# Lower left quarter of the diagonal score blocks read back from memory instead of computed; pairs in a new order, steps of the row work moved

## The chip, the cores and the metric

The kernel runs on one core of one Trainium2 chip. The metric is the device time of one execution in microseconds (us); the median of several runs counts.

## What is computed

For each of 8 batches of 2496 rows: scores of z with itself, squared after a Relu, applied to v, and multiplied by u elementwise. The result x (19968 rows of 256) goes through a mixture of 8 experts, each of which takes at most 80 rows.

```python
scores = (1.0 / S) * np.matmul(z, z.transpose(0, 2, 1))     # 8 x 2496 x 2496
attn = np.maximum(scores, 0.0) ** 2
x = (u * np.matmul(attn, v)).reshape(B * S, D)
logits = x @ w_gate                                        # 19968 x 8
expert_idx = np.argmax(logits, axis=1)                     # gate_w: its softmax share
for e in range(E):                                         # the 80 rows of largest gate_w
    h = np.maximum(x[tok_idx] @ w1[e], 0.0)
    out[tok_idx] = gate_w[tok_idx, None] * (h @ w2[e])
```

The score matrix of a batch is symmetric, since both factors are z.

## The kernel before

The rows of a batch are 20 tiles of 128 (the last holds 64), and five query chunks `qc` of four tiles: 512 columns, 448 in the last. A chunk is worked off against ten key pairs (two tiles of keys each), so a batch is a grid of five by ten steps, and the program is a list of 400 steps `(b, qc, r)`, r being the position in `pairs_of`. For each step `attend` does the products with v: for both tiles of the pair and both halves of the 256 output columns three matmuls (high and low parts, `ah`, `al` of the scores and the two parts of v), all adding into the chunk's accumulators; the batch's last tile needs two of the three. Two steps earlier (`LOOK`), `scores` prepares the pair: where key chunk and query chunk are equal or the keys come later, PE computes them (two matmuls a tile: `zc` and `zd` hold the parts of z), ACT does Relu and square, ACT or DVE casts the high part `ah`, and DVE subtracts for the low part `al`.

Where the key chunk is later, the scores are kept for the mirrored block too. `mirror` transposes 32 by 32 blocks on DVE into a tile `x`, `mirror_out` writes it to memory (`y`, 1 MB for 512 by 512), `mirror_back` reads it transposed at the level of blocks into one of four buffers (`blk`, four DMAs), and `mirrored` takes the high and low parts of a pair from there with a copy on ACT and a subtract on DVE. So only 240 of the 400 pairs are computed; the two pairs of a diagonal block (`k // QT == qc`) always are, in full.

While a chunk runs, `finished` does the row work of the chunk before it, each part at a step number `r` of its own: `chunk_x` multiplies by u at the start, then high, middle and low parts for the logits (`xb`), `chunk_store` (two DMA transposes of x from SP), `chunk_store2` (the write of x), `chunk_logits` and `chunk_sum`, and once per batch the gate (`gate_top`, `gate_sum`), the counts and the table. The same loop loads and prepares z and v of the next batch (`load_z`, `prep_zc`, `load_v`, `prep_v`). PE, ACT, DVE and SP run in the order in which this loop writes their instructions. After the last chunk come the choice of rows and the experts.

The lines on which the steps turn (before):

```python
pairs_of = [list(range(NP)) for qc in range(NQ)]
pairs_of[NQ - 2] = [NP - 2, NP - 1, *range(NP - 2)]
...
nc.tensor.matmul(s[:, :nq], zk, zc[:, :nq], start=True, stop=False)
nc.tensor.matmul(s[:, :nq], zk, zd[:, :nq], start=False, stop=True)
```

Of the kernel before, what the change touches and what calls it, by code (L numbers as in the profile page):

```python
# [25 lines left out]
def attn_moe_kernel(ctx, tc, zT, uT, v, wg, w1, w2, out, seq, cap):  # L26
# [26 lines left out]
    def tt(o, a, b, op):  # L53
        V.tensor_tensor(out=o, in0=a, in1=b, op=op)  # L54
# [172 lines left out]
    nsum = const.tile([P, B + 1], F32, name="nsum")  # L227
    tot = const.tile([P, E, NBLK], F32, name="tot")
    incl = const.tile([P, E, NBLK], F32, name="incl")
# [6 lines left out]
    def zero_out(i, n):  # L236
# [8 lines left out]

    pairs_of = [list(range(NP)) for qc in range(NQ)]
    pairs_of[NQ - 2] = [NP - 2, NP - 1, *range(NP - 2)]
    LOOK, AHEAD = 2, 12
# [7 lines left out]

    to_read = [(b, i, j, (b * NQ + i) * NP + pairs_of[i].index(2 * j) - LOOK)
               for b in range(B) for i in range(NQ) for j in range(i)]
# [20 lines left out]
    def mirror_back():  # L279

        while to_read and free:
# [12 lines left out]
            blk[b, i, j] = m  # L294

    def pair_tile(tag, b, qc, k, dt=F32R, bufs=3):
        return ew.tile([P, 2, CH], dt, tag=tag, name=f"{tag}_{b}_{qc}_{k}", bufs=bufs)
# [17 lines left out]
    def scores(b, qc, k):  # L315

        if k // QT < qc:
            return mirrored(b, qc, k)
        nq = min(CH, seq - qc * CH)
        zc, zd = zc_t[b, qc], zd_t[b, qc]  # L320
        a = pair_tile("a", b, qc, k, F32, 2)
        ss = []
        for h in range(2):
            zk = zc_t[b, k // QT][:, (k % QT + h) * P:(k % QT + h + 1) * P]
            s = ps_s.tile([P, CH], F32, tag="s", name=f"s_{b}_{qc}_{k + h}")
            nc.tensor.matmul(s[:, :nq], zk, zc[:, :nq], start=True, stop=False)  # L326
            nc.tensor.matmul(s[:, :nq], zk, zd[:, :nq], start=False, stop=True)  # L327
            ss.append(s)
        for h, s in enumerate(ss):
            nc.scalar.activation(out=a[:, h, :nq], in_=s[:, :nq], func=AF.Relu)  # L330
        nc.scalar.activation(out=a[:, :, :nq], in_=a[:, :, :nq], func=AF.Square)  # L331
        ah = pair_tile("ah", b, qc, k)
        on_v = k // QT == qc or (qc, k) in ON_V and b > 0
        cp(V if on_v else nc.scalar, ah[:, :, :nq], a[:, :, :nq])
        al = pair_tile("al", b, qc, k)
        tt(al[:, :, :nq], a[:, :, :nq], ah[:, :, :nq], ALU.subtract)
        if k // QT > qc:
            for h in range(2):
                mirror(b, k // QT, qc, k % QT + h, a[:, h])
        a_t[b, qc, k] = (ah, al)  # L340
# [3 lines left out]
    def attend(b, qc, k, cols=range(DC)):  # L344
        nq = min(CH, seq - qc * CH)
        first, last = 2 * pairs_of[qc][0], 2 * pairs_of[qc][-1] + 1
        if k == first:
# [116 lines left out]
    def gate_top(b, q0, q1):  # L464
# [16 lines left out]
        tt(d, lg, bc(mx), ALU.subtract)  # L481
        ex = ex_last[:, q0 * QT:q1 * QT] if last else small("ex")
        nc.scalar.activation(out=ex, in_=d, func=AF.Exp)
# [202 lines left out]
    WARM = 3, 6  # L686
    WARM0 = 8
    steps = [(b, qc, r) for b in range(B) for qc in range(NQ) for r in range(NP)]
    ET = mybir.EngineType
# [31 lines left out]
    def finished(b, qc, r):  # L721
# [4 lines left out]
        elif r == 2:  # L726
            chunk_rest(b, qc)
        if r == (3 if at_end else 1):
            chunk_store(b, qc)
        if r == (5 if at_end else 3):  # L730
            chunk_store2(b, qc)
        if r == (2 if at_end else 3):
            chunk_mid(b, qc)
        if r == (3 if at_end else 4):
            chunk_lo(b, qc)
        if r == (5 if at_end else 6):
            chunk_logits(b, qc)
            chunk_sum(b, qc)
        kb = b * BPB
        if b < B - 1 and qc == NQ - 1:  # L740
            if r == 7:
                gate_top(b, 0, NQ)
            elif r == 8:
                gate_sum(b, gate_near(b, 0), gp)
        elif qc == 0 and b > 0:
            part = kb - BPB, kb
            if r == 2:
                count(*part)
            elif r == 4:
                up_to(*part)  # L750
                blocks(ps_m, "m", gp, oh, *part)
# [13 lines left out]
    with tc.manual_schedule(engines={ET.PE, ET.Activation, ET.DVE, ET.SP}):  # L765
# [11 lines left out]
        for i, (b, qc, r) in enumerate(steps):  # L777
# [4 lines left out]
            if i + LOOK < len(steps):  # L782
                nb, nqc, nr = steps[i + LOOK]
                scores(nb, nqc, 2 * pairs_of[nqc][nr])
            if r == 0 and prev:
                chunk_x(*prev)
            if b == 0 and qc == 0:
# [5 lines left out]
                if r == 8:  # L793
                    constants_v()
            p = pairs_of[qc][r]
            for k in (2 * p, 2 * p + 1):
# [8 lines left out]
            if b + 1 < B:  # L805
                if r == 1:
                    z_raw[b + 1, qc] = load_z(b + 1, qc)
                if r == 5:
                    prep_zc(b + 1, qc, z_raw.pop((b + 1, qc)))
                if qc == NQ - 2 and r in (2, 4):  # L810
                    g = r // 2 - 1
                    v_raw[b + 1, g] = load_v(b + 1, g)
                if qc == NQ - 1:
                    g = (r - 1) // 2 if r < 9 else 4
                    if r in (2, 4, 6, 8, 9):
                        prep_v(b + 1, g, v_raw.pop((b + 1, g)), nc.scalar, V)
                        if g + 2 < NQ:
                            v_raw[b + 1, g + 2] = load_v(b + 1, g + 2)
            if nb < B and r == 1:
                prep_zd(nb, nqc)  # L820
# [6 lines left out]
            mirror_back()  # L827
            mirror_out()
            if r == NP - 1:
                prev = b, qc  # L830
# [580 lines left out]
```

## Time and profile before

| | |
|---|---|
| median of 3 runs (lowest to highest) | 1389.96 us (1388.79 to 1390.28) |
| the profiled execution | 1388.46 us |
| its span, first to last instruction | 1386.6 us |
| PE busy | 1367.1 us, 99% |
| DVE, ACT busy | 1060.6 us (76%), 1008.8 us (73%) |
| mean granted TensorE clock | 0.992 of full |
| DMA | 311.89 MB, mean 225 GB/s |

The span is what the profile sees; the execution is 1.9 us longer. The stream of attention matmuls begins at 10.0 us and ends near 1305; a batch takes 162.0 us of it. In the rows below PE is TensorE, PEld its weight loads, DVE VectorE, ACT ScalarE, SP the engine that issues most DMAs. A row of the timeline gives start, length, engine, line, operation, output and input.

### The profile page before, as it was taken

Reading aid. Unit: us, or ns where it says so; the run is one execution under the profiler, and the core shown is the slowest. Engines: PE = TensorE matmul, PEld = TensorE weight load, DVE = VectorE, ACT = ScalarE, POOL = GpSimd, SP = SyncE. Lnnn points to the kernel's source line nnn. Section 1 sums busy time; section 2 is a strip of 40 time slices with the busy share of each in tenths; the row PEclk is TensorE's granted clock in tenths of the full one; section 3 lists DMA queues with packets and bytes.
Section 4 is the critical chain, followed back from the end, with each engine's and each line's share of the span. In section 5 each row is a group of like instructions: output and inputs, shape, how many; then the busy total and the mean of one; then the engine's idle time right before and its main releaser. Section 6 shows DMA issues by size and latency. Waiting matters only on the chain. (4 is left out here: it accounts for less than half of the span.)

```text
span 1386.6 us, 19562 instructions
## 1 busy us (share of the span) xinstructions
PE 1367.1 (99%) x7087; PEld 1139.5 (82%) x7087; DVE 1060.6 (76%) x1517; ACT 1008.8 (73%) x1282; POOL 36.5 (3%) x57
## 2 busy tenths in 40 slices
PE   9999999999999999999999999999999999999887
PEld 6888888888888888888888888888888888888666
DVE  8876788668877788767886688777787678867785
ACT  8866687758777587666887577775877668876375
POOL 0000000000000000000000000000000000000062
PEclk9999999999999999999999999999999999999989
DMA  6899877995888958997688958889588986789774
GB/s 223 252 249 271 225 204 239 235 267 143 256 237 231 273 151 245 239 261 197 188 252 232 270 143 259 238 225 274 145 246 239 255 210 179 220 229 252 176 225 141
DMA packets 260070, 311.89 MB, mean 225 GB/s; under 512 B 96152, under 2 KB 188192, under 8 KB 249728
## 3 DMA queue, kind: packets, MB, share of 16 engines
q1 hardware_dynamic: 258752, 309.02, 81.4%
q0 software_dynamic: 1216, 1.56, 0.4%
q8 instruction: 57, 0.93, 0.3%
q14 instruction: 45, 0.37, 0.1%
HBM read 153.48 MB, written 126.37 MB: 202 GB/s over the span
## 5 line engine op out<-in xcount | busy, mean ns | idle before, releaser
L359 PE MATMUL acc<-ah,vt 128*128 128x512 f32 (+1 forms) x1520 | 584.5, 385 | 0.3 <-DVE vt L146 0.3
L360 PE MATMUL acc<-al,vt 128*128 128x512 f32 (+1 forms) x1520 | 584.5, 385 | 0.3 <-DVE al L54 0.2
L358 PE MATMUL acc<-ah,vt 128*128 128x512 f32 (+1 forms) x1520 | 584.2, 384 | 0.0
L54 DVE TENSOR_TENSOR al<-a,ah 128x1024 fp32r<-128x1024 f32 (+1 forms) x240 | 291.5, 1214 | 135.4 <-ACT ah L105 125.6
L330 ACT ACTIVATE a<-s 128x512 f32<-128x512 f32 (+1 forms) x480 | 258.4, 590 | 153.9 <-PE s L327 143.8
L359 PEld LDWEIGHTS acc<-ah,vt 128*128 128x128 f32 x1520 | 285.4, 188 | 53.9 <-DVE vt L146 1.2
L358 PEld LDWEIGHTS acc<-ah,vt 128*128 128x128 f32 x1520 | 285.3, 188 | 52.9
L360 PEld LDWEIGHTS acc<-al,vt 128*128 128x128 f32 x1520 | 285.4, 188 | 52.9 <-DVE al L54 1.2
L331 ACT ACTIVATE a<-a 128x1024 f32<-128x1024 f32 (+1 forms) x240 | 253.0, 1054 | 7.6
L310 ACT CAST ah<-blk 128x1024 fp32r<-128x1024 f32 x160 | 167.0, 1049 | 105.6 <-PE acc L359 88.5
L54 DVE TENSOR_TENSOR al<-blk,ah 128x1024 fp32r<-128x1024 f32 x160 | 193.8, 1216 | 56.1 <-ACT ah L310 53.2
L265 DVE STREAM_TRANSPOSE x<-a 128x512 f32<-128x512 f32 x320 | 207.6, 687 | 0.0
L327 PE MATMUL s<-zd,zc 128*128 128x512 f32 (+1 forms) x480 | 186.5, 388 | 0.0
L105 ACT CAST ah<-a 128x1024 fp32r<-128x1024 f32 x153 | 160.9, 1052 | 4.8
L107 DVE CAST ah<-a 128x1024 fp32r<-128x1024 f32 (+1 forms) x87 | 59.2, 681 | 95.6 <-ACT a L331 95.6
L326 PE MATMUL s<-zc,zc 128*128 128x512 f32 x320 | 128.1, 400 | 0.0
L327 PEld LDWEIGHTS s<-zd,zc 128*128 128x128 f32 x480 | 90.3, 188 | 16.3 <-issue 0.5
L326 PEld LDWEIGHTS s<-zc,zc 128*128 128x128 f32 x320 | 60.1, 188 | 11.1
L326 PE MATMUL s<-zc 128*128 128x512 f32 (+1 forms) x160 | 63.5, 397 | 0.0
L388 ACT CAST xb<-xf 128x1024 bf16<-128x1024 f32 (+1 forms) x39 | 40.0, 1026 | 23.4 <-DVE xf L377 23.1
L396 ACT CAST xb<-xr 128x1024 bf16<-128x1024 f32 (+1 forms) x39 | 39.9, 1024 | 15.5 <-DVE xr L54 15.5
L377 DVE SCALAR_TENSOR_TENSOR xf<-acc,ut 128x512 f32<-128x512 f32 (+2 forms) x82 | 50.1, 653 | 0.0
(171 smaller groups left out, 835.9 us busy)
## 6 DMA issues: line engine op xcount, KB each, us to landing
y<-x SPq DMA_DIRECT2D x80, 1024.0 KB
blk<-y SPq DMA_DIRECT2D x320, 256.0 KB
out<-idle SPq DMA_DIRECT2D x40, 512.0 KB
vraw<-v SPq DMA_DIRECT2D x32, 512.0 KB
ut<-uT SPq DMA_DIRECT2D x32, 512.0 KB
xs<-xq SPq DMA_DIRECT2D x32, 512.0 KB
wraw<-w SPq DMA_DIRECT2D x28, 512.0 KB
zd<-zc SPq DMA_DIRECT2D x78, 128.0 KB
```

Of the source, the lines that this page charges most:

```text
L54: V.tensor_tensor(out=o, in0=a, in1=b, op=op)
L105: eng.copy(out=o, in_=i)
L107: eng.tensor_copy(out=o, in_=i)
L265: V.transpose(out=x[:, :, :, t].rearrange("p n k s -> p k n s"), in_=a)
L310: nc.scalar.copy(out=natural(ah), in_=src)
L326: nc.tensor.matmul(s[:, :nq], zk, zc[:, :nq], start=True, stop=False)
L327: nc.tensor.matmul(s[:, :nq], zk, zd[:, :nq], start=False, stop=True)
L330: nc.scalar.activation(out=a[:, h, :nq], in_=s[:, :nq], func=AF.Relu)
L331: nc.scalar.activation(out=a[:, :, :nq], in_=a[:, :, :nq], func=AF.Square)
L358: nc.tensor.matmul(o, vt[:, t, 0, cs], ah, start=k == first, stop=False)
L359: nc.tensor.matmul(o, vt[:, t, 1, cs], ah, start=False, stop=False)
L360: nc.tensor.matmul(o, vt[:, t, 0, cs], al, start=False, stop=k == last)
```

## The change

A diagonal block is symmetric in itself. Of its two pairs the first (tiles 0 and 1 of the chunk as keys) is still computed in full, and the right half of its result, columns 256 on, is the mirror image of the left half of the second pair. `quarter_out` transposes that right half in 32 by 32 blocks on DVE (tile `xd`), `quarter_write` writes it to memory two steps later (`yd`, 0.25 MB), `quarter_back` reads it after step 3 (`md`, four DMAs of 32 partitions, pieces of 128 values), and the second pair computes columns 256 on alone and takes the rest from `md` by a copy on ACT and a subtract on DVE. `xd` and `md` share one buffer. The first block of the first batch and the last block of the last batch are computed whole as before.

A chunk now starts with its first diagonal pair and ends with its second. x's DMA transposes move from step 1 to 4, its write from 3 to 6, the logits from 6 to 7 (not for the last chunk), the gate, the counts and the table by one to five steps. Key chunks of the next batch are loaded one chunk later, and of v's five groups the last is prepared in the next batch's first chunk. `tot` becomes bfloat16, and the exponentials of the gate overwrite the logits.

```diff
     gall = const.tile([P, NCOL - NT + 32], F32, name="gall")
     nsum = const.tile([P, B + 1], F32, name="nsum")
-    tot = const.tile([P, E, NBLK], F32, name="tot")
+    tot = const.tile([P, E, NBLK], BF16, name="tot")
     incl = const.tile([P, E, NBLK], F32, name="incl")
...
-    pairs_of = [list(range(NP)) for qc in range(NQ)]
-    pairs_of[NQ - 2] = [NP - 2, NP - 1, *range(NP - 2)]
+    def whole_block(b, qc):
+        return (b, qc) in ((0, 0), (B - 1, NQ - 1))
+    def order(b, qc):
+        rest = [p for p in range(NP) if p // 2 != qc]
+        if whole_block(b, qc):
+            return list(range(NP))
+        if qc == NQ - 2:
+            rest = rest[-2:] + rest[:-2]
+        return [2 * qc, *rest, 2 * qc + 1]
+    pairs_of = {(b, qc): order(b, qc) for b in range(B) for qc in range(NQ)}
+    HQ = CH // 2
     LOOK, AHEAD = 2, 12
...
             blk[b, i, j] = m
+    quarter = {}
+    def quarter_out(b, qc, a):
+        x = zpool.tile([P, n32, 2, 2, SQ], F32, tag="md", name=f"xd_{b}_{qc}", bufs=1)
+        for t in range(2):
+            V.transpose(out=x[:, :, :, t].rearrange("p n k s -> p k n s"), in_=a[:, t, HQ:])
+        quarter[b, qc] = now[0], x
+    def quarter_write():
+        for (b, qc), (at, x) in list(quarter.items()):
+            if at is not None and at + 2 <= now[0]:
+                y = dram.tile([n32, SQ, n32, 4 * SQ], F32, tag="yd", name=f"yd_{b}_{qc}", bufs=2)
+                nc.sync.dma_start(out=y.rearrange("g p h f -> (g p) (h f)"),
+                                  in_=x.rearrange("p h k t s -> p (h k t s)"))
+                quarter[b, qc] = None, y
+    def quarter_back(b, qc):
+        _, y = quarter.pop((b, qc))
+        m = zpool.tile([P, n32, 2, 2 * SQ], F32, tag="md", name=f"md_{b}_{qc}", bufs=1)
+        for h in range(n32):
+            nc.sync.dma_start(out=m[h * SQ:(h + 1) * SQ].rearrange("p g k f -> p g (k f)"),
+                              in_=y[:, :, h].rearrange("g p f -> p g f"))
+        quarter[b, qc] = None, m
     def pair_tile(tag, b, qc, k, dt=F32R, bufs=3):
...
         nq = min(CH, seq - qc * CH)
         zc, zd = zc_t[b, qc], zd_t[b, qc]
+        diag = k // QT == qc and not whole_block(b, qc)
+        lower = diag and k % QT > 0
+        c0, c1 = (HQ, nq) if lower else (0, CH if diag else nq)
         a = pair_tile("a", b, qc, k, F32, 2)
...
             zk = zc_t[b, k // QT][:, (k % QT + h) * P:(k % QT + h + 1) * P]
             s = ps_s.tile([P, CH], F32, tag="s", name=f"s_{b}_{qc}_{k + h}")
-            nc.tensor.matmul(s[:, :nq], zk, zc[:, :nq], start=True, stop=False)
-            nc.tensor.matmul(s[:, :nq], zk, zd[:, :nq], start=False, stop=True)
+            nc.tensor.matmul(s[:, c0:c1], zk, zc[:, c0:c1], start=True, stop=False)
+            nc.tensor.matmul(s[:, c0:c1], zk, zd[:, c0:c1], start=False, stop=True)
             ss.append(s)
         for h, s in enumerate(ss):
-            nc.scalar.activation(out=a[:, h, :nq], in_=s[:, :nq], func=AF.Relu)
-        nc.scalar.activation(out=a[:, :, :nq], in_=a[:, :, :nq], func=AF.Square)
+            nc.scalar.activation(out=a[:, h, c0:c1], in_=s[:, c0:c1], func=AF.Relu)
+        nc.scalar.activation(out=a[:, :, c0:c1], in_=a[:, :, c0:c1], func=AF.Square)
         ah = pair_tile("ah", b, qc, k)
+        al = pair_tile("al", b, qc, k)
+        if lower:
+            m = quarter.pop((b, qc))[1].rearrange("p n k (t s) -> p k t n s", t=2)
+            def natural(o):
+                return o[:, :, :HQ].rearrange("p k (t n s) -> p k t n s", t=2, s=SQ)
+            nc.scalar.copy(out=natural(ah), in_=m)
+            tt(natural(al), m, natural(ah), ALU.subtract)
         on_v = k // QT == qc or (qc, k) in ON_V and b > 0
-        cp(V if on_v else nc.scalar, ah[:, :, :nq], a[:, :, :nq])
-        al = pair_tile("al", b, qc, k)
-        tt(al[:, :, :nq], a[:, :, :nq], ah[:, :, :nq], ALU.subtract)
+        cp(V if on_v else nc.scalar, ah[:, :, c0:nq], a[:, :, c0:nq])
+        tt(al[:, :, c0:nq], a[:, :, c0:nq], ah[:, :, c0:nq], ALU.subtract)
+        if diag and not lower:
+            quarter_out(b, qc, a)
         if k // QT > qc:
...
         d = d_last if q1 == NQ and last else small("d")
         tt(d, lg, bc(mx), ALU.subtract)
-        ex = ex_last[:, q0 * QT:q1 * QT] if last else small("ex")
+        ex = ex_last[:, q0 * QT:q1 * QT] if last else lg
         nc.scalar.activation(out=ex, in_=d, func=AF.Exp)
...
     WARM = 3, 6
     WARM0 = 8
+    keys_in = {qc: [(qc - 1, 1, 6)] for qc in range(1, NQ)}
+    keys_in[0] = []
+    keys_in[NQ - 1] = [(NQ - 2, 1, 4), (NQ - 1, 4, 7)]
     steps = [(b, qc, r) for b in range(B) for qc in range(NQ) for r in range(NP)]
...
         elif r == 2:
             chunk_rest(b, qc)
-        if r == (3 if at_end else 1):
+        if r == (3 if at_end else 4):
             chunk_store(b, qc)
-        if r == (5 if at_end else 3):
+        if r == (5 if at_end else 6):
             chunk_store2(b, qc)
...
         if r == (3 if at_end else 4):
             chunk_lo(b, qc)
-        if r == (5 if at_end else 6):
+        if r == (5 if at_end else 6 if qc == NQ - 1 else 7):
             chunk_logits(b, qc)
...
         kb = b * BPB
         if b < B - 1 and qc == NQ - 1:
-            if r == 7:
+            if r == 8:
                 gate_top(b, 0, NQ)
-            elif r == 8:
+            elif r == 9:
                 gate_sum(b, gate_near(b, 0), gp)
         elif qc == 0 and b > 0:
             part = kb - BPB, kb
-            if r == 2:
+            if r == 7:
                 count(*part)
-            elif r == 4:
+            elif r == 9:
                 up_to(*part)
...
                 prep_u(b, qc)
             if b + 1 < B:
-                if r == 1:
-                    z_raw[b + 1, qc] = load_z(b + 1, qc)
-                if r == 5:
-                    prep_zc(b + 1, qc, z_raw.pop((b + 1, qc)))
+                for j, load, prep in keys_in[qc]:
+                    if r == prep:
+                        prep_zc(b + 1, j, z_raw.pop((b + 1, j)))
+                    if r == load:
+                        z_raw[b + 1, j] = load_z(b + 1, j)
                 if qc == NQ - 2 and r in (2, 4):
...
                     v_raw[b + 1, g] = load_v(b + 1, g)
                 if qc == NQ - 1:
-                    g = (r - 1) // 2 if r < 9 else 4
-                    if r in (2, 4, 6, 8, 9):
+                    if r in (1, 3, 6, 8):
+                        g = (1, 3, 6, 8).index(r)
                         prep_v(b + 1, g, v_raw.pop((b + 1, g)), nc.scalar, V)
                         if g + 2 < NQ:
                             v_raw[b + 1, g + 2] = load_v(b + 1, g + 2)
+            if b and qc == 0 and r == 3:
+                prep_v(b, NQ - 1, v_raw.pop((b, NQ - 1)), nc.scalar, V)
             if nb < B and r == 1:
...
             mirror_back()
             mirror_out()
+            quarter_write()
+            if r == 3 and not whole_block(b, qc):
+                quarter_back(b, qc)
             if r == NP - 1:
```

What the order of the instructions shows, at three places of the second batch's second chunk (`qc` 1, whose diagonal pairs are tiles 4, 5 and 6, 7).

On PE, the score matmuls of the diagonal block's second pair; `s_1_6` and `s_1_7` are the scores of tiles 6 and 7. Before, between the products of tiles 0, 1 and tiles 2, 3:

```order
L359 MATMUL acc_1_1_3648<-ah_1_0_3580,vt_0_3062 128x512
L360 MATMUL acc_1_1_3648<-al_1_0_3582,vt_0_3062 128x512
L326 MATMUL s_1_6_3662<-zc_1_2286 128x512
L327 MATMUL s_1_6_3662<-zd_1_3341,zc_1_2286 128x512
L326 MATMUL s_1_7_3665<-zc_1_2286 128x512
L327 MATMUL s_1_7_3665<-zd_1_3341,zc_1_2286 128x512
L358 MATMUL acc_1_0_3647<-ah_1_2_3612,vt_0_3062 128x512
```

Of the change, between the products of tiles 14, 15 and tiles 16, 17:

```order
L410 MATMUL acc_1_1_3764<-ah_1_14_3890,vt_3_3348 128x512
L411 MATMUL acc_1_1_3764<-al_1_14_3891,vt_3_3348 128x512
L367 MATMUL s_1_6_3984<-zc_1_2696 128x256
L368 MATMUL s_1_6_3984<-zd_1_3445,zc_1_2696 128x256
L367 MATMUL s_1_7_3987<-zc_1_2696 128x256
L368 MATMUL s_1_7_3987<-zd_1_3445,zc_1_2696 128x256
L409 MATMUL acc_1_0_3763<-ah_1_16_3924,vt_4_3511 128x512
```

The four matmuls moved from the chunk's second step to its eighth and have 256 columns instead of 512.

On DVE, the end of the first chunk and the start of the second; `lg` and `mx` to `oh` are the gate of the finished batch, `al_1_0` the low part of the first mirrored pair of chunk 1, `al_0_18` the last full pair of chunk 0. Before:

```order
L54 TENSOR_TENSOR al_0_18_3545<-a_0_18_3533,ah_0_18_3543 128x1024
L265 STREAM_TRANSPOSE x_4_0_3492<-a_0_18_3533 128x4x4x32 x2
L478 TENSOR_REDUCE mx_0_3561<-lg_2346 128x20
L54 TENSOR_TENSOR d_0_3563<-lg_2346,mx_0_3561 128x160
L486 SCALAR_TENSOR_TENSOR fw_0_3567<-d_0_3563,first_w 128x160
L489 TENSOR_REDUCE mf_0_3569<-fw_0_3567 128x20
L490 TENSOR_TENSOR oh<-fw_0_3567,mf_0_3569 128x10x2x8
L494 MEMSET oh 64x4
L54 TENSOR_TENSOR al_1_0_3582<-blk_1_0_3471,ah_1_0_3580 128x1024
```

Of the change, to the gate's third instruction (`al_1_0` follows right behind the gate, as before):

```order
L54 TENSOR_TENSOR al_0_18_3602<-a_0_18_3591,ah_0_18_3601 128x1024
L276 STREAM_TRANSPOSE x_4_0_3575<-a_0_18_3591 128x4x4x32 x2
L510 TENSOR_REDUCE lg_2426<-pl_4_3621 128x32
L54 TENSOR_TENSOR al_0_2_3660<-md_0_3517,ah_0_2_3659 128x2x256
L107 CAST ah_0_2_3659<-a_0_2_3649 128x2x256
L54 TENSOR_TENSOR al_0_2_3660<-a_0_2_3649,ah_0_2_3659 128x2x256
L107 CAST ah_1_4_3692<-a_1_4_3682 128x1024
L54 TENSOR_TENSOR al_1_4_3693<-a_1_4_3682,ah_1_4_3692 128x1024
L313 STREAM_TRANSPOSE xd_1_3696<-a_1_4_3682 128x2x4x32 x2
L529 TENSOR_REDUCE mx_0_3709<-lg_2426 128x20
L54 TENSOR_TENSOR d_0_3711<-lg_2426,mx_0_3709 128x160
L537 SCALAR_TENSOR_TENSOR fw_0_3714<-d_0_3711,first_w 128x160
```

The lower pair of chunk 0 (`al_0_2`, from `md_0` and from `a_0_2`) and the first diagonal pair of chunk 1 with its transposes (`xd_1`) now stand ahead of the gate.

On SP, the DMAs of the second chunk, up to the first mirrored block of the third. Before:

```order
L427 DMA_TRANSPOSE xq_0_5239<-xf_0_5193 128x8x128 x2
L100 DMA zraw_5242<-zT 128x512
L120 DMA zd_2_5244<-zc_2_4139 64x512
L121 DMA zd_2_5244<-zc_2_4139 64x512
L159 DMA ut_1_5281<-uT 128x2x512
L436 DMA xs<-xq_0_5239 128x8x256
L580 DMA wtab<-wb_5357 80x256
L239 DMA out<-idle 128x4x256
L275 DMA y_2_1_5392<-x_2_1_5261 128x2048
L292 DMA blk_2_1_5478<-y_2_1_5392 32x4x512 x4
```

Of the change:

```order
L321 DMA yd_1_5387<-xd_1_5306 128x512
L100 DMA zraw_5419<-zT 128x512
L120 DMA zd_2_5421<-zc_2_4601 64x512
L121 DMA zd_2_5421<-zc_2_4601 64x512
L159 DMA ut_1_5453<-uT 128x2x512
L330 DMA md_1_5485<-yd_1_5387 32x4x128 x4
L478 DMA_TRANSPOSE xq_0_5518<-xf_0_5368 128x8x128 x2
L286 DMA y_2_1_5522<-x_2_1_5403 128x2048
L239 DMA out<-idle 128x4x256
L487 DMA xs<-xq_0_5518 128x8x256
L303 DMA blk_2_1_5586<-y_2_1_5522 32x4x512 x4
```

The quarter's write and four reads (`yd_1`, `md_1`) are new, and x's transposes stand behind them instead of first.

## Rows read from the trace of the kernel before

**Rows 1.** The page's busy times, us and share of the span.
```profile
PE 1367.1 (99%) x7087; PEld 1139.5 (82%) x7087; DVE 1060.6 (76%) x1517; ACT 1008.8 (73%) x1282; POOL 36.5 (3%) x57
```

**Rows 2.** Batch 3 by chunk: length, busy per engine, clock, DMA share, GB/s.
```profile
495.88:530.60 34.72, 34.72 (x176) 28.67 (x174) 29.16 (x43) 28.65 (x39) 0.00 (x0) 1.00 0.65 180
530.60:564.88 34.28, 34.28 (x176) 28.06 (x175) 29.20 (x52) 27.44 (x37) 0.00 (x0) 1.00 0.85 252
564.88:599.60 34.72, 34.72 (x175) 28.68 (x174) 23.34 (x29) 26.70 (x34) 0.00 (x0) 1.00 0.93 236
599.60:628.88 29.28, 29.28 (x151) 24.18 (x150) 20.27 (x22) 15.27 (x18) 0.00 (x0) 1.00 0.98 274
628.88:657.88 29.00, 29.00 (x163) 26.44 (x162) 22.61 (x25) 21.30 (x27) 0.00 (x0) 1.00 0.72 194
sum 162.00, PE 162.00 PEld 136.04 DVE 124.58 ACT 119.36 POOL 0.00; mean PE 32.40 PEld 27.21 DVE 24.91 ACT 23.87 POOL 0.00
```

**Rows 3.** Timeline of PE, first and last matmul of three runs.
```profile
599.83 0.39 PE L359 MATMUL acc<-ah,vt 128*128 128x512 f32 x1
...
614.79 0.39 PE L358 MATMUL acc<-ah,vt 128*128 128x512 f32 x1
...
1294.79 0.36 PE L359 MATMUL acc<-ah,vt 128*128 128x448 f32 x1
...
1299.86 0.36 PE L359 MATMUL acc<-ah,vt 128*128 128x448 f32 x1
...
1340.05 0.28 PE L1196 MATMUL op<-w2h,hTh 128*80 128x256 f32 x1
...
1342.74 0.28 PE L1196 MATMUL op<-w2h,hTl 128*80 128x256 f32 x1
```

**Rows 4.** Timeline of PEld, loads of 128 and of 80 columns.
```profile
1301.06 0.19 PEld L358 LDWEIGHTS acc<-ah,vt 128*128 128x128 f32 x1
1301.17 0.19 PEld L359 LDWEIGHTS acc<-ah,vt 128*128 128x128 f32 x1
...
1340.05 0.15 PEld L1196 LDWEIGHTS op<-w2l,hTh 128*80 128x80 f32 x1
1340.17 0.15 PEld L1196 LDWEIGHTS op<-w2h,hTl 128*80 128x80 f32 x1
```

**Rows 5.** The page's costliest matmuls, and the idle time before them.
```profile
L359 PE MATMUL acc<-ah,vt 128*128 128x512 f32 (+1 forms) x1520 | 584.5, 385 | 0.3 <-DVE vt L146 0.3
```

**Rows 6.** Groups by shape: busy us, mean ns of one, idle before.
```profile
L54 DVE TENSOR_TENSOR al<-a,ah 128x1024 fp32r<-128x1024 f32 x224 | 274.0, 1223 | 134.2 <-ACT ah L105 125.6 <-DVE ah L107 0.5
L330 ACT ACTIVATE a<-s 128x512 f32<-128x512 f32 x448 | 242.8, 594 | 132.3 <-PE s L327 122.2 <-DVE x L265 8.2
...
L265 DVE STREAM_TRANSPOSE x<-a 128x512 f32<-128x512 f32 x320 | 207.6, 687 | 0.0
...
L310 ACT CAST ah<-blk 128x1024 fp32r<-128x1024 f32 x160 | 167.0, 1049 | 105.6 <-PE acc L359 88.5 <-PE acc L362 9.7 <-DMA blk<-y 5.0
...
L107 DVE CAST ah<-a 128x1024 fp32r<-128x1024 f32 x71 | 49.2, 693 | 84.1 <-ACT a L331 84.1
```

**Rows 7.** Timeline of ACT, DVE and PE in batch 3's first chunk.
```profile
514.20 1.08 ACT L330 ACTIVATE a<-s 128x512 f32<-128x512 f32 x2
...
517.38 1.09 ACT L330 ACTIVATE a<-s 128x512 f32<-128x512 f32 x2
...
514.33 1.22 DVE L54 TENSOR_TENSOR al<-a,ah 128x1024 fp32r<-128x1024 f32 x1 [1.82 <-ACT ah L105]
...
517.64 0.39 PE L358 MATMUL acc<-ah,vt 128*128 128x512 f32 x1
...
529.40 1.23 DVE L54 TENSOR_TENSOR al<-blk,ah 128x1024 fp32r<-128x1024 f32 x1 [0.19 <-ACT ah L310]
...
531.05 0.39 PE L360 MATMUL acc<-al,vt 128*128 128x512 f32 x1
```

**Rows 8.** Waits, of ACT and of SP's queue: us, times, longest.
```profile
ACT ah L310 <- DMA blk<-y: 5.0, 7, 1.7
...
SPq L292 <- DMA y<-x: 179.5, 38, 8.7
```

More of the change, by code (lines that the diff above doesn't have):

```diff
@@ L255, in attn_moe_kernel @@
     now, to_write = [0], []
-    to_read = [(b, i, j, (b * NQ + i) * NP + pairs_of[i].index(2 * j) - LOOK)
+    to_read = [(b, i, j, (b * NQ + i) * NP + pairs_of[b, i].index(2 * j) - LOOK)
                for b in range(B) for i in range(NQ) for j in range(i)]
@@ L345, in attend @@
         nq = min(CH, seq - qc * CH)
-        first, last = 2 * pairs_of[qc][0], 2 * pairs_of[qc][-1] + 1
+        first, last = 2 * pairs_of[b, qc][0], 2 * pairs_of[b, qc][-1] + 1
         if k == first:
@@ L783, in attn_moe_kernel @@
                 nb, nqc, nr = steps[i + LOOK]
-                scores(nb, nqc, 2 * pairs_of[nqc][nr])
+                scores(nb, nqc, 2 * pairs_of[nb, nqc][nr])
             if r == 0 and prev:
@@ L794, in attn_moe_kernel @@
                     constants_v()
-            p = pairs_of[qc][r]
+            p = pairs_of[b, qc][r]
             for k in (2 * p, 2 * p + 1):
```

## The prediction, made before the changed kernel was run

> **What bounds the kernel now.** I read the busy totals first: TensorE (PE) is busy for 99% of the span [rows 1]. That is not proof by itself, since the ends of matmuls are modelled, so I looked for waits. The costliest matmul line, 1520 matmuls, sat idle before them for 0.3 us in all [rows 5]. I then cut one batch of the middle (batch 3) into its five query chunks. PE is busy from edge to edge in each, at granted clock 1.00, while DVE is busy for 124.58 and ACT for 119.36 of the 162.00 us [rows 2]. The DMA engines come nearest to PE there: 0.93 and 0.98 of the third and fourth chunk, but 0.65 and 0.72 of the first and fifth [rows 2]. So the eight batches are a stream of matmuls without gaps, and a microsecond of matmul taken out of it is a microsecond off the span, as long as nothing that feeds PE becomes late.
>
> The rate of that stream comes from starts, since durations overlap: 66 matmuls of 512 columns start between the two rows at 599.83 and 614.79, so one costs 226.7 ns; 25 of 448 columns take 5.07 us, 202.8 ns each; 23 of 256 columns, in the expert part, take 2.69 us, 117.0 ns each [rows 3]. (At 1.00 clock; a step of one pair is 12 accumulating matmuls, 2.72 us, and with four score matmuls 3.63 us.)
>
> **What the change removes from PE.** In 38 of the 40 diagonal blocks the second pair computes only its right part. 31 of these blocks are of 512 columns: four score matmuls each go from 512 to 256 columns. What 256 columns cost behind a load of 128 weight columns no row shows directly. From below: the 117.0 ns of the expert part, whose loads have 80 columns. From above: nothing saved beyond what the 448-column row has, 202.8 ns, if the weight load of 188 ns that the profile gives (0.19 in [rows 4]) has to end before the next matmul starts. I take 120 ns, near the lower end, for two reasons in the rows: two loads of 128 columns start 0.11 us apart (1301.06 and 1301.17), and loads of 80 columns, recorded at 0.15 us, start every 0.12 us, so a recorded load runs on beside the next one [rows 4]. That gives 31 x 4 x (226.7 - 120) = 13.2 us. In seven blocks of the last chunk the pair goes from 448 to 192 columns; by the load spacing that can't be below 107 ns, and I take 112: 7 x 4 x (202.8 - 112) = 2.5 us. Their first pair, on the other hand, now computes 512 columns instead of 448: 7 x 4 x 23.9 ns = 0.7 us back. Sum: 15.1 us (15.6 with 117 and 107; 2.3 with 202.8 throughout).
>
> The number of matmuls stays the same, and so does everything on PE outside the scores; logits and counts only change their step. The first block and the last are computed whole as before, and so are the start and the tail of 80 us after the stream; I cost them at nothing.
>
> **What it adds, and what hides it.** *DVE*, per block: two transposes of 256 columns (half of the 687 ns row each, 0.7 us), one subtract more but both of half size (no change beyond some 0.1 us), a cast of half size (0.3 us less): about 0.5 us [rows 6]. *ACT*: a copy of 512 elements per partition from the mirrored quarter (half of 1049 ns) against halves of two Relu passes of 594 ns and of the square: between 0.6 us less and, if no pass got shorter at all, 0.5 us more [rows 6]. With 37 and 43 us free per batch [rows 2], both lie beside PE on average. Where they don't have slack on average is what counts, so I looked at the two tightest places.
>
> First, the change from the first chunk to the second, where the gate of the finished batch sits on DVE. The low part of that block's first pair ends at 529.40 + 1.23 = 530.63 and PE uses it at 531.05: 0.42 us to spare, the smallest margin of a batch [rows 7]. Between the start of the block's last tile pair and that use PE does one step before, of ten accumulating matmuls (2.27) and four score matmuls (0.91). Now the lower pair and the next diagonal pair stand between on DVE (0.6 + 0.4 + 0.6 and 0.7 + 1.2 + 0.7 = 4.2 us, from [rows 6] and the parts above), but PE does three steps there: 2.27, 3.63 and 2.72, 8.6 us instead of 3.2. The margin grows by 5.4 - 4.2 = 1.2 us.
>
> Second, the last value group's preparation moves into the first chunk's fourth step. It is three ACT copies of 1280 elements together, 1.3 us at the 1049 ns row. ACT starts a pair every 3.18 us there (514.20 to 517.38) against PE's 3.63, so it wins 0.45 us a step, and the pair of that stretch ends its low part at 515.55, 2.1 us before PE's step at 517.64 [rows 7]. 1.3 us fits, and is won back in three steps. If it did not fit, the excess would show in each of seven batches.
>
> *DMA*: per block one write and four reads, 0.25 MB each way; 2.6 MB per batch. The stream moves 36.7 MB per batch in 133.7 us of DMA time (share x length over [rows 2]), 275 GB/s, so 9.5 us more if the small pieces run at that rate and 19 at half of it: 143 to 153 of 160 us. It fits on average, and not in the fourth chunk, which has 0.6 us free; what overflows goes into the fifth, which has 8. What could be late there: the read of the quarter is issued at step 3, used by ACT at step 7 and by PE at step 9. SP stands still at a read whose write hasn't landed: the existing mirror does that 38 times, 4.7 us on average, 8.7 at worst, with two steps in between [rows 8]; the quarter has three steps and a quarter of the bytes, so I expect less. Behind it in SP's queue stand x's transposes, the next z chunk, a zero-fill and the store of x; first to be missed would be z (for the key chunk three steps on), then the mirrored blocks. But the mirrored blocks of a chunk are all used one step later than before (2.4 to 3.6 us), which is more than the 0.5 MB (1.9 us) that now goes ahead of them, and ACT's waits for them were 5.0 us in the whole span [rows 8]. x's transposes, moved to step 4, still have six steps (over 14 us) until the next chunk overwrites x; logits one step later have two until the gate. All of this I cost at nothing.
>
> **The sum.** The profiled execution took 1388.46 us for a span of 1386.6; less 15.1 this gives 1373.4. The median of the runs is 1389.96, 1.5 above that execution, so the median after should be about 1374.9. Its own range is 1372 to 1378.
>
> **Rivals.** *Short matmuls that don't get shorter* (0.08). If a matmul can't start until the 188 ns load is over, 256 columns cost what 448 do, 2.3 us are saved, and the time is 1387.7: no change that can be told. For it: 448 columns at 202.8 ns is 188 plus 15, as if bound by the load. Against it: the 117 ns cadence beside recorded loads of 150. The Trainium skill's page "TensorE: Matmul & The Clock Gate", section "Back-to-back issue gap", gives a sustained roofline of about 131 ns at 512 columns and 81 at 128, from which 256 columns would save only some 33 ns (an estimate by interpolation), 4 us in all. This trace doesn't agree with it: 226.7 ns at 512 columns.
>
> *ACT or DVE eat part of it* (0.13). The place is the first chunk, whose ACT gets 1.3 us more within one step; if pair chains there run late by 1 us beyond the margin, 7 batches cost 7 us and the time is 1382; between 1378 and 1387.
>
> *DMA becomes the bound, slower* (0.07). The place is the fourth and fifth chunk of a batch. If the quarter's write needs the fourteen microseconds that the worst mirror write needed (two steps and 8.7 us) and SP holds back z and the mirrored blocks behind it, PE waits in both chunks. It gains nothing from 1.1 us of wait in each of 14 such chunks and loses beyond it; at 2 us each the time is 1374.9 + 28 = 1403. For it: 0.98 [rows 2]. Against it: 8 us free right behind, and deadlines that moved later too.
>
> **How the numbers follow.** My forecast has 0.72. Within 0.2% (2.8 us) is about what a measurement of this kernel can't tell from no change. Forecast and second rival are faster, 0.85; the first rival is the same, 0.08; the last is slower, 0.07. The range of 8 in 10 takes the forecast and most of the second rival: 1371 to 1386.
>
> **What would show it.** Right: score matmuls of 256 columns starting about 120 ns apart; the five chunks of a batch together 160.0 us instead of 162.0, 1.7 us of it in the first four; PE still busy from edge to edge; ACT's copy of the quarter without waits for DMA. Wrong: 200 ns between these starts; or PE idle before an accumulating matmul, with ACT's copy named as the one that came last and SP waiting at the quarter's read; or idle time in each first chunk, behind the moved preparation of v. The prediction fails if any wait of half a microsecond appears in every block: 38 such waits are worth more than the saving.

## The result and the profile after

The changed kernel takes 1407.0 us (median of 5 runs, 1403.77 to 1408.77), the kernel before 1389.58 beside it: ratio 1.013 (95% interval 1.0118 to 1.0141), so 1.3% slower and clear of the noise, where 1374.9 and faster was predicted. The profiled execution took 1403.77 us for a span of 1402.0, 15.4 more than before.

The page's busy times after, for [rows 1]:

```profile
PE 1364.2 (97%) x7087; PEld 1137.2 (81%) x7087; DVE 1078.8 (77%) x1631; ACT 993.9 (71%) x1320; POOL 37.6 (3%) x57
```

PE's share fell from 99% to 97%: there are gaps now. Batch 3 by chunk, for [rows 2] (same columns):

```profile
500.07:534.35 34.28, 34.28 (x175) 28.39 (x174) 28.84 (x41) 27.87 (x40) 0.00 (x0) 1.00 0.86 250
534.35:573.29 38.94, 36.28 (x180) 29.74 (x179) 30.44 (x53) 28.25 (x38) 0.00 (x0) 0.96 0.66 199
573.29:607.73 34.44, 34.44 (x178) 28.49 (x176) 23.95 (x37) 25.39 (x34) 0.00 (x0) 1.00 0.93 227
607.73:636.61 28.88, 28.88 (x152) 23.90 (x150) 21.18 (x27) 16.11 (x21) 0.00 (x0) 1.00 1.01 277
636.61:664.45 27.84, 27.84 (x159) 25.38 (x158) 22.86 (x28) 19.99 (x25) 0.00 (x0) 1.00 1.04 263
```

Four chunks are shorter than before and full from edge to edge. The second lost 4.66 us: PE is idle for 2.66 of it, and the mean granted clock is 0.96. So the place is known; the timeline of the changed kernel there shows the event, PE first, then DVE and ACT:

```profile
558.83 0.28 PE L367 MATMUL s<-zc 128*128 128x256 f32 x1
558.95 0.28 PE L368 MATMUL s<-zd,zc 128*128 128x256 f32 x1
559.07 0.28 PE L367 MATMUL s<-zc 128*128 128x256 f32 x1
559.19 0.28 PE L368 MATMUL s<-zd,zc 128*128 128x256 f32 x1
...
562.06 0.77 PE L502 MATMUL pl<-wgs,xb 128*128 128x24 bf16 x24
565.48 0.23 PE L588 MATMUL tp<-oh,ones_b 128*128 128x80 bf16 x2 [2.66 <-DVE lg L510]
...
566.68 0.63 PE L409 MATMUL acc<-ah,vt 128*128 128x512 f32 x1
567.11 0.63 PE L410 MATMUL acc<-ah,vt 128*128 128x512 f32 x1
...
562.38 0.38 DVE L112 CAST zc<-zraw 128x512 fp32r<-128x512 f32 x1
562.80 0.69 DVE L54 TENSOR_TENSOR zc<-zraw,zc 64x512 fp32r<-64x512 f32 x1
563.50 0.69 DVE L54 TENSOR_TENSOR al<-md,ah 128x512 fp32r<-128x512 f32 x1
564.11 0.42 DVE L107 CAST ah<-a 128x512 fp32r<-128x512 f32 x1
564.57 0.69 DVE L54 TENSOR_TENSOR al<-a,ah 128x512 fp32r<-128x512 f32 x1
565.18 0.25 DVE L510 TENSOR_REDUCE lg<-pl 128x32 f32<-128x96 f32 x1
...
565.75 0.23 ACT L590 CAST tot<-tp 128x80 bf16<-128x80 f32 x1 [4.03 <-PE tp L588]
```

The logits (`pl`, L502) and the count of the finished batch (`tp`, L588) are both in step 7 of a batch's second chunk now, and both take their PSUM tile (the memory into which matmuls write) from the pool `ps_m`, which has one buffer. So the count's first matmul has to wait until DVE has read the logits (the reduce, L510). That reduce stands in DVE's queue behind the key chunk's preparation and the three operations of the lower pair, and ends at 565.43. PE works in order: all that is behind the count waits too. Afterwards matmuls of 512 columns start 0.427 us apart instead of 0.227, for a while. The windows of the wait and behind it (clock in the third column from the right):

```profile
562.06:565.48 3.42, 0.76 (x26) 0.69 (x25) 3.28 (x7) 0.00 (x0) 0.00 (x0) 1.00 0.88 364
565.48:566.68 1.20, 1.20 (x7) 0.98 (x6) 0.00 (x0) 0.63 (x2) 0.00 (x0) 0.88 0.28 116
566.68:570.43 3.75, 3.75 (x11) 2.95 (x10) 1.76 (x2) 1.89 (x4) 0.00 (x0) 0.58 0.00 0
```

PE was at 2.4 GHz (granted clock 1.00), did nothing for 2.66 us, and then its matmuls came at the pace of 1.2 GHz for some 3.6 us (mean granted clock 0.58 in the last window). The waits of the whole span, for [rows 8] (us, times, longest), and the costliest matmul, for [rows 5]:

```profile
SPq L303 <- DMA y<-x: 75.9, 24, 8.2
...
ACT ah L381 <- DMA md<-yd: 27.2, 15, 5.2
...
PE tp L588 <- DVE lg L510: 17.4, 7, 2.7
```

```profile
L409 PE MATMUL acc<-ah,vt 128*128 128x512 f32 (+1 forms) x1520 | 588.0, 387 | 1.9 <-DVE ah L107 1.9
```

The count's wait comes seven times, once for every batch but the first. The first of two small matmuls at each count carries the wait, and the costly line [rows 5] shows nothing of it: its 1.9 us are another wait, in the last batch.

Two theories stood before the runs below. Theory A: the loss is the wait for the one buffer, and the clock behind the wait. Theory B: the quarter's way through memory makes DVE and ACT late, and the count only shows it.

### The profile page after: what moved, and what is told of

Its sections match the earlier page's. It is cut to its first block, busy times and chain, and to the rows that moved or that the text cites. A ratio compares the mean times of both kernels' runs of the same rounds, so it can differ in the third digit from the quotient of the medians.

```text
span 1402.0 us, 19932 instructions
## 1 busy us (share of the span) xinstructions
PE 1364.2 (97%) x7087; PEld 1137.2 (81%) x7087; DVE 1078.8 (77%) x1631; ACT 993.9 (71%) x1320; POOL 37.6 (3%) x57
## 5 line engine op out<-in xcount | busy, mean ns | idle before, releaser
L54 DVE TENSOR_TENSOR al<-a,ah 128x1024 fp32r<-128x1024 f32 (+1 forms) x240 | 271.2, 1130 | 142.4 <-ACT ah L105 137.8
L371 ACT ACTIVATE a<-s 128x512 f32<-128x512 f32 x480 | 243.3, 557 | 118.1 <-PE s L368 113.6
L372 ACT ACTIVATE a<-a 128x1024 f32<-128x1024 f32 x240 | 237.5, 989 | 7.8
L368 PE MATMUL s<-zd,zc 128*128 128x512 f32 x480 | 179.8, 378 | 0.0
L367 PE MATMUL s<-zc,zc 128*128 128x512 f32 x320 | 124.7, 390 | 0.0
L107 DVE CAST ah<-a 128x1024 fp32r<-128x1024 f32 (+3 forms) x87 | 48.7, 559 | 51.4 <-ACT a L372 51.0
L54 DVE TENSOR_TENSOR al<-md,ah 128x512 fp32r<-128x512 f32 x38 | 26.1, 686 | 42.2 <-ACT ah L381 40.4
L367 PE MATMUL s<-zc 128*128 128x512 f32 (+3 forms) x160 | 58.5, 376 | 0.0
```

Source lines behind the costliest of these rows:

```text
L107: eng.tensor_copy(out=o, in_=i)
L367: nc.tensor.matmul(s[:, c0:c1], zk, zc[:, c0:c1], start=True, stop=False)
L368: nc.tensor.matmul(s[:, c0:c1], zk, zd[:, c0:c1], start=False, stop=True)
L371: nc.scalar.activation(out=a[:, h, c0:c1], in_=s[:, c0:c1], func=AF.Relu)
L372: nc.scalar.activation(out=a[:, :, c0:c1], in_=a[:, :, c0:c1], func=AF.Square)
```

## Experiments

Ratios are to the kernel before, run beside each; brackets are 95% intervals. (7,3) is batch 7, chunk 3. Unless another kernel is named, an edit is one of the changed kernel.

**Count back in step 2.** `if r == 7: count` to `r == 2`, the table from step 9 to 4.

> The changed kernel with one thing undone: the counts of the finished batch go back from step 7 to step 2 of the second chunk, their sums and table from step 9 to step 4. Theory A (the counts' matmuls wait for the one PSUM buffer that the logits of the same step hold until DVE has summed them, 2.7 us a batch, and the granted clock falls behind the wait, 1.4 us more; about 4 us in each of seven batches): the wait goes, the second chunk takes about 35.0 us instead of 38.9, the time is 1376 to 1381, below the kernel before. Theory B (the quarter's way through memory keeps DVE and ACT late, and the counts only show it): PE waits as long elsewhere, the time stays at 1400 or above.

Measured: 1378.7 us, ratio 0.9927 [0.9915, 0.9939]. The second chunk takes 35.07 us in batch 3.

**Count one step after the logits.** `if r == 7: count` to `r == 8`.

> The changed kernel, the counts one step later (8 instead of 7), sums and table at 9 as in the change. Theory A: one step is 2.7 to 3.6 us, and DVE's sum of the logits ended 2.5 us after the logits' last matmul, so the counts find the buffer free or nearly so: at most 0.5 us of wait a batch, the time is 1376 to 1384. Theory B: as before, 1400 or above.

Measured: 1377.29 us, 0.9919 [0.9904, 0.9933]; second chunk 34.66, batch 3 160.10 us. With the count in step 2 and in step 8 alike it starts without a wait in all seven batches, as theory A has it.

**No quarter.** `diag = False`, no `quarter_back`: lower pairs computed whole, all else of the change kept.

> The changed kernel without the mirrored quarter: the second diagonal pair is computed whole, so there are no transposes for it, no write, no reads; the order of pairs and all moved steps stay. Theory A: the 15 us of score columns come back and the wait of the counts stays (DVE has the same work ahead of the logits' sum, to 0.1 us), so the time is 1415 to 1425. Theory B: without the transfers the stall is gone, and the time is that of the kernel before, 1387 to 1393.

Measured: 1403.41 us, 1.0116 [1.0094, 1.0138]. Without any quarter the kernel is still slow, so B is not the loss. But it was less than expected of A: the wait is 1.87 us in four batches, and behind a wait that long the clock stayed at 1.00. The wait is shorter from both sides: in batch 3, counted from the start of the second chunk, PE comes to the logits at 28.11 us instead of 27.71 and DVE ends the reduce at 30.68 instead of 31.08. The lower pair's own work on DVE isn't shorter: from its first operation to the reduce 1.94 us, against 1.68 with the quarter. In batches 1 and 6 the wait is 2.2 us; the clock fell behind the first of these and not behind the second. The windows behind the count in batches 1, 2 and 6:

```profile
237.38:241.38 4.00, 4.00 (x14) 3.16 (x14) 0.95 (x2) 2.37 (x4) 0.00 (x0) 0.65 0.01 2
402.90:406.90 4.00, 4.00 (x19) 3.34 (x19) 0.94 (x2) 3.06 (x5) 0.00 (x0) 1.00 0.02 4
1058.74:1062.74 4.00, 4.00 (x19) 3.32 (x19) 0.94 (x2) 3.03 (x5) 0.00 (x0) 1.00 0.02 8
```

**The kernel before, with only the collision.** In the old kernel: logits from step 6 to 7, count from 2 to 7, table from 4 to 9.

> The kernel before with only this moved: logits of all but the last chunk from step 6 to 7, counts from step 2 to 7, sums and table from 4 to 9. Nothing of the quarter, old order of pairs, old place of x's transposes. Theory A: the counts wait behind the logits here too (DVE has a subtract and two transposes ahead of the sum, 2.4 us), with the clock's fall some 3 to 4.5 us in seven batches, so the time is 1408 to 1421. Theory B: no quarter, no stall: 1388 to 1392.

Measured: 1409.55 us, 1.0147 [1.0132, 1.0162]. This alone makes a slowdown of 20.7 us, in a kernel without any of the quarter. In batches 1 and 2, windows of the wait and of the 4 us behind it:

```profile
235.80:237.99 2.19, 0.01 (x2) 0.00 (x0) 2.13 (x4) 0.00 (x0) 0.00 (x0) 1.00 1.02 313
237.99:241.99 4.00, 4.00 (x13) 3.15 (x13) 1.22 (x1) 1.19 (x2) 0.00 (x0) 0.60 0.80 166
401.63:403.82 2.19, 0.00 (x1) 0.00 (x1) 2.13 (x4) 0.00 (x0) 0.00 (x0) 1.00 0.99 352
403.82:407.82 4.00, 4.00 (x19) 3.34 (x19) 1.28 (x2) 2.24 (x3) 0.00 (x0) 1.00 0.91 190
```

Equal waits, but 13 matmuls behind the one and 19 behind the other: these second chunks take 37.98 and 36.36 us. The fall of the clock costs 1.6 us of its own where it comes, in four of the seven batches.

**The wait filled with matmuls on idle data.** Behind the logits of each first chunk, which PE computes during the second:

```diff
+        if qc == 0 and b > 0:
+            for _ in range(14):
+                nc.tensor.matmul(pl[:, P:], idle[:, :P], idle[:, :CH - P], start=True, stop=True)
```

> The changed kernel, with 14 matmuls of 384 bf16 columns on idle data placed on PE behind the logits of each second chunk's hold (the count in step 7 still waits for the reduce of the logits, and nothing is left out of the computation; the added matmuls write PSUM columns that nobody reads). They should take some 2.2 to 2.4 us, about as long as PE's wait in the changed kernel. The theory that the loss is the wait plus a clock that falls behind it: the wait stays as long in sum, the granted clock in the stretch behind the count stays at 1.00, the matmuls there stand 0.227 us apart in place of 0.427, and each of the seven batches wins 1.4 to 2.0 us: 1391 to 1397 us. The rival, that the whole loss is the wait and what must be caught up behind it: the second chunk stays at 38 to 39 us and the time at 1403 to 1409 us.

Measured: 1395.16 us, 1.0055 [1.0039, 1.007]. Timeline of PE:

```profile
558.01 2.44 PE L507 MATMUL pl<-idle 128*128 128x384 bf16 x14
560.80 0.23 PE L591 MATMUL tp<-oh,ones_b 128*128 128x80 bf16 x2 [0.36 <-DVE lg L513]
...
561.87 0.39 PE L409 MATMUL acc<-ah,vt 128*128 128x512 f32 x1
562.10 0.39 PE L410 MATMUL acc<-ah,vt 128*128 128x512 f32 x1
```

The count starts as late as before, the matmuls behind it stand 0.23 us apart, the chunk takes 37.31 us, 1.63 less than in the changed kernel. So the wait and the clock are two costs, and this is the first alone.

**A buffer of its own**, that is, one of the three of the scores' pool, which the logits don't use. `tp = ps_m.tile(..., tag="m")` in `count` to `ps_s.tile(..., tag="s")`; step 7 kept.

> The changed kernel, count left in step 7, but its PSUM tile taken from the pool of the scores (three buffers) in place of the pool that the logits use (one buffer). If the loss is that one buffer is shared by the logits and the count: PE no longer waits for the reduce (0 of the 2.66 us), the second chunk takes 34.6 to 35.3 us, and the time is 1376 to 1381 us, as with the count in another step. If the count's step 7 is in itself the trouble (too much work in it for DVE or ACT, whatever buffer): 1400 us or more.

Measured: 1375.57 us, 0.9908 [0.9893, 0.9923]. Its batch 3, second chunk and sum:

```profile
524.06:558.58 34.52, 34.52 (x180) 28.52 (x179) 29.26 (x49) 28.14 (x38) 0.00 (x0) 1.00 0.76 222
...
sum 159.97, PE 159.97 PEld 134.68 DVE 127.89 ACT 117.40 POOL 0.00; mean PE 31.99 PEld 26.94 DVE 25.58 ACT 23.48 POOL 0.00
```

The step isn't the trouble; the shared buffer is.

**x's transposes back at step 1** (store at 3), on the kernel with the count in step 8: the old lines of the diff in `finished`. From here on the question is why the quarter is late for ACT. Theory C: x's transposes, which go out right behind the quarter's read, slow it.

> The changed kernel with the count in step 8 (1377.3 us when it ran), and the DMA transposes of x and the store behind them back in steps 1 and 3, where they stood before the change (in the last but one chunk of the last batch they stay in steps 3 and 5). Theory C, that the lower quarter's read back is late for ACT because its packets stand behind the DMA transposes issued right after it: ACT's waits for md in the fourth and fifth chunks (0.6 to 3.7 us) go away in batches 0 to 6 and that of 5.1 us in (7,3) stays; PE lost only about 0.1 us to the former, so the time is 1376.3 to 1378.5 us. The rival, that the transposes in step 1 stand in the way of the quarter's write and of the mirrored blocks: fourth or second chunks become longer, 1380 us or more.

Measured: 1423.42 us, 1.0239 [1.022, 1.0258]: a large miss, on the rival's side. SP's queue in the fourth chunk of batch 3, which starts at 610.57:

```profile
608.38 0.34 SPq L321 DMA_DIRECT2D yd<-xd  x1
616.65 2.64 SPq L478 DMA_TRANSPOSE xq<-xf  x2
619.34 0.57 SPq L100 DMA_DIRECT2D zraw<-zT  x1
...
626.27 6.97 SPq L330 DMA_DIRECT2D md<-yd  x4
```

DVE and ACT there:

```profile
615.97 1.25 DVE L428 SCALAR_TENSOR_TENSOR xf<-acc,ut 128x512 f32<-128x512 f32 x2
...
638.63 0.62 ACT L381 CAST ah<-md 128x512 fp32r<-128x512 f32 x1 [7.72 <-DMA md<-yd]
```

SP's queue in the kernel with the count in step 8 (chunk from 593.45):

```profile
605.70 3.88 SPq L330 DMA_DIRECT2D md<-yd  x4
610.25 5.11 SPq L478 DMA_TRANSPOSE xq<-xf  x2
```

At step 1 the transposes stand in SP's queue until DVE has made `xf`, and everything behind them with them: the quarter's read goes out 15.7 us into the chunk instead of 12.25. Its four DMAs then also take longer to issue, 6.97 us instead of 3.88; why, no run tells. ACT waits for it 7.72 us there, and the eight fourth chunks are 4.7 to 6.7 us longer each, 45 us in all.

**Late transposes at the end.** In the kernel with the count in step 8, `at_end`'s store from steps 3 and 5 to 5 and 7.

> The changed kernel with the count in step 8 (1377.3 us), and the DMA transposes of x of chunk (7,3) alone moved from step 3, just behind the quarter's read back, to step 5 (the store behind them from 5 to 7). Theory C: md is there 3 to 5 us earlier, PE does not wait for it, chunk (7,3) takes 28.9 to 29.5 us in place of 31.31, and the time is 1374.9 to 1375.9 us. The rival, that md is late in (7,3) by the load of the queue as a whole (weights of the last stage, mirrored blocks): (7,3) stays at 31 us and the time at 1377 us, or worse where x arrives late for the last stage.

Measured: 1378.58 us, 0.9927 [0.9914, 0.9941]; (7,3) takes 31.75 us. The edit missed its place: `at_end` belongs to the chunk that is finished during (7,4). So the run says nothing on theory C. The next three, on the kernel with the buffer of its own, are about the same chunk (7,3), which takes 31.63 us there against 29.28 before.

**The last quarter's write first.** `quarter_write()` also called ahead of `weights_ahead`. Theory D: the quarter's write is late in (7,3), behind a load of weights in SP's queue.

> The kernel with the count in a buffer of its own (1375.57 us), and the write of chunk (7,3)'s lower quarter issued on SP one place earlier, ahead of a load of the last stage's weights; nothing else moves. In the trace of that kernel the weights' load waits 9.6 us for DVE to free its buffer, the quarter's write stands behind it (issued at 1241.86 us, 8.3 us after the chunk began), and ACT waits for the quarter's read. Theory D, head of SP's queue: the write goes out some 8 to 10 us earlier, ACT's wait for md in (7,3) goes from 5 us to 0 to 1, the chunk takes 28.9 to 29.5 us in place of 31.63, the time is 1372.9 to 1374.0 us. Theory C, the transposes behind the read back: the read is still followed by the transposes, so (7,3) stays above 30.5 us.

Measured: 1377.8 us, 0.9919 [0.9906, 0.9933]; chunk 30.71. The write went out at 1231.94 as meant, but ACT still waits 4.53 us: D explains 0.9 of the 2.35 us in this chunk, and a gain in the time can't be told: from the start of the last chunk to the end of the span the kernel with the buffer of its own takes 108.50 us and this one 110.46, more of a difference than the chunk makes.

**The transposes behind.** For chunk (7,2): `chunk_store` in step 6, `chunk_store2` in step 8.

> The kernel with the count in a buffer of its own (1375.57 us), and the DMA transposes of x that are issued in chunk (7,3) (those of chunk (7,2)) moved from step 4 to step 6 there, behind four mirrored blocks and a load of weights; this is the edit that the earlier run with late transposes meant to make (it moved those issued in the chunk after). Theory C: md is in 2 to 4 us earlier and (7,3) takes 29 to 30 us, the time 1373 to 1374.3 us. Theory D: the write of the quarter is as late as before, (7,3) stays within 0.7 us of 31.6 us and the time within 1374.5 to 1376.6 us.

Measured: 1379.48 us, 0.9931 [0.9917, 0.9944]; chunk 32.08. The transposes went out at 1261.61 and the quarter was there at 1262.2, no earlier: C falls for this chunk.

**The last quarter not used.** `whole_block` also true for (7,3), its order kept.

> The kernel with the count in a buffer of its own (1375.57 us), and the diagonal block of chunk (7,3) alone computed whole, in the same order of pairs: no quarter to write, read or wait for there, for four matmuls of 512 columns in place of 256. If the 2.3 us that this chunk is above 28.87 + 0.43 us are md's lateness and nothing else: 29.2 to 29.4 us, and the time 1373.2 to 1374.3 us. If something else in that chunk (weights split on ACT and DVE) holds PE: 30.5 us or more, and 1375 to 1376.5 us.

Measured: 1373.82 us (1372.39 to 1374.43), 0.989 [0.9875, 0.9905], the lowest median of all; (7,3) in its trace:

```profile
1234.06:1263.41 29.35, 28.69 (x148) 23.34 (x146) 23.54 (x25) 19.07 (x22) 0.00 (x0) 1.00 0.94 237
```

That is 2.28 us less than with the quarter, though four matmuls have 512 columns again, so most of what the chunk had lost was the quarter's lateness. PE still waits 0.66 us in it, for another pair.

## Why the prediction was wrong

**The step that failed** is "logits and counts only change their step", which put the move at nothing; of the logits the part on DMA says it again ("All of this I cost at nothing."). I counted DMAs, ACT and DVE at their new places but did not ask which buffer the two use. What the runs show in its place is PE's wait for that one buffer, and the lower clock behind it. Against the 34.52 us of the kernel with a buffer of its own, the seven second chunks after are 28.7 us longer. In that kernel the count starts 0.62 us after the logits, in batch 3 after the change 3.42: 2.8 us late, in six batches, and 1.63 us in the last. That makes 18.4; the other 10.3 lie behind six of the waits, where the clock is lower. The span after is 28.3 us above that kernel's.

**The matmuls of 256 columns**: right. Four start at 558.83, 558.95, 559.07 and 559.19: 120 ns. My estimate of a saving of only some 33 ns for each, interpolated from the sustained figures of the Trainium skill's page "TensorE: Matmul & The Clock Gate", section "Back-to-back issue gap", does not hold here: 226.7 less 120 is 107.

**The sum of 15.1 us**: right in size. Batch 3 was to take 160.0 us; it takes 159.97 with the count's own buffer. Over that kernel's span 12.9 us of it are left (1386.6 to 1373.7), since (7,3) is 2.35 us longer than before; with that block whole it is 15.0 us by the medians (1388.82 to 1373.82). From the first attention matmul to the start of the last chunk, which leaves out a tail that differs from run to run, the two kernels save 11.6 and 14.2 us. The places were not those of the prediction: of batch 3's 2.0 us, 0.9 come in the first four chunks, not 1.7, and 1.2 in the fifth. The new order moves four score matmuls from the fifth chunk to the second (20 and 28 of them before, 16 and 32 after), which I had not counted.

**ACT and DVE in the first chunk**: right, no chunk (b,0) lost anything (34.28 us). What I took for DVE's slack I worked out for `al` alone. The reduce in the rows on the order of DVE's queue is that of the last chunk's logits, ahead of a lower pair; the one that mattered comes a chunk later, and the timeline above has it behind the lower pair.

**"ACT's copy of the quarter without waits for DMA"**: wrong, 27.2 us in 15 waits, but of PE's waits only one of 1.9 us, in (7,3), comes from them. The rival in which DMA makes the kernel slower had 1403 us, close to the 1407.0 measured, but that is chance: it had PE wait in the fourth and fifth chunks, and those take 28.9 and 27.85 us, less than before, but for two fourth chunks (29.19 us in batch 6, 31.36 in batch 7). A loss of that kind was avoided by an order that I had not costed: with x's transposes at their old step the fourth chunks lose 45 us, behind the head of SP's queue.

**What stays open**: why the quarter is late in (7,3). Neither the write's place nor the transposes explain more than 0.9 us. The traces point at the read itself. In the kernel with the buffer of its own it goes out 15.24 us into (7,3), and 12.24 to 12.36 us into the seven other fourth chunks; ahead of it in SP's queue stands a second load of weights, which had to wait 1.6 us for DVE (in the trace, with the chunk from 1233.60):

```profile
1245.95 0.39 SPq L665 DMA_DIRECT2D wraw<-w  x1
...
1248.84 3.73 SPq L330 DMA_DIRECT2D md<-yd  x4
```

Neither edit moved this load: with the write first the read goes out at 15.26 us, with the transposes behind at 15.23. That the load is the cause is not shown; an earlier read there was not tried.

## What to carry to other kernels

When a step is moved, list the buffers that it takes, who had them last, and how late in a queue that release stands; a pool of one buffer turns two cheap steps into a wait of an in-order engine. A DMA that waits for data at the head of a queue delays what stands behind it, so a transfer with a short deadline goes ahead of it. And a gap in PE's stream can cost more than its length: here 1.3 to 2.8 us more in six batches of seven.

## What the runs showed of the hardware

The clock behind a gap was not a matter of the gap's length alone. After 2.19 us of idle PE, matmuls of 512 columns stood 0.427 us apart in batch 1 and 0.227 in batch 2 of the same execution (the old kernel with the collision); in that kernel all seven waits are 2.18 or 2.19 us long, and four of them had slow matmuls behind them. After 2.66 us (six times) they were slow each time, after some 1.87 us (four times, without the quarter) never. With matmuls on idle data in place of most of the gap, none was slow.
